# Rebuilding the last stage of a linear-attention, gated-MLP and soft-MoE kernel: turns by VectorE, experts in landing order, two output banks

## Chip, cores and metric

The kernel runs on one core of one Trainium2 chip (trn2). The metric is the device time of one execution in microseconds. The kernel before took 850.67 us, the median of three runs (848.72 to 850.92).

## What is computed

A linear attention over 8 batches of 8 heads gives x (4608 rows, 512 columns); a gated MLP with 1536 inner columns follows; and last a soft mixture of 8 experts with 4 slots each. Only the last part is touched:

```python
logits = x @ phi                              # 4608 x 32
d = softmax of logits over the 4608 rows
slot_input = d.T @ x                          # 32 x 512, 4 rows per expert
for e in range(8):
    h = np.maximum(slot_input[e] @ w1[e], 0)  # 512 -> 1024
    slot_out[e] = h @ w2[e]                   # 1024 -> 512
c = softmax of logits over the 32 slots       # the combine weights
out = c @ slot_out
```

All of it is float32. Each expert has 4 MB of weights, 33.5 MB in all, and the output is 9.4 MB.

## The kernel before, in words

The order of all instructions is written out by hand: `PROGRAM` is a list of steps such as `pair 9 2` or `piece 18`, and each mention of a step runs its generator to its next `yield`. Every engine (PE, VectorE, ScalarE, POOL, and the DMA queues of SP and POOL) works its share of this list strictly in order, so a step that waits holds back whatever stands behind it on its engine. The rows are cut into ten blocks, 0 to 7 of 512 rows and 8 and 9 of 256.

For each block, `pair(n, i)` (L591) makes one of 12 tiles of 128 inner columns of the MLP: products into g and v (L601), Silu on ScalarE (L608), product on VectorE (L610). These pairs are the bulk of PE's work. The MLP's output product is never formed: phi and w_out are folded into `wp` at the start, and `logits` (L655) takes the logits straight from the tiles hT.

`post_a` to `post_d` (L672 to L750) are the two softmaxes. `post_a` copies the logits out of PSUM, and `post_b` sums and replicates them by a product with `rep` (L690 for the last block), takes the running maximum (L697 to L701), the Exp (L705), turns the result in 32x32 blocks with VectorE into dN (L720), and turns the logits into `c_sb`, one row per token (L726). `post_d` makes the combine weights of it in place. `post_c` multiplies dN with the turned tiles hN (L763, called dh) and updates the sum U (L771).

After the last block, U is turned (`u_end`, L932), multiplied with w_out (`slot_in`, L941, tile si, 12 products of 512 columns), scaled in two halves out of one PSUM bank (L950, L952) and turned into siT (L956, L960).

The experts come next. `ex_a` (L964) multiplies siT with w1 into four column groups of one bank (L971, 256 columns), then Relu on ScalarE (L982); `ex_b` turns the result with PE (L989) and places the expert's four columns into h1T, which is zero elsewhere (L995); `ex_c` (L998) adds up y over all experts in one bank (L1007), in products of 512 columns, two column groups to a half piece. `c_stack_a` and `c_stack_b` (L781, L790) split the combine weights into a high and a low part, both twice, and turn them with PE (L798) into cT with 128 rows. `fin_a` and `fin_b` copy y, sum its four column groups by a product with `rep` (so, L1032) and split it the same way into st. `emit(k)` (L1038) then makes 512 output rows with four products of 128 rows in fp32r (L1045), copies them out alternately with ScalarE and VectorE (L1048, L1050), and writes each half, 512 KB, by SP (L1053).

The experts' weights are loaded in half pieces of 512 KB by POOL's DMA queue (`load_half`, L816; 64 in all). A piece goes where memory comes free, by the list `PLACE` (L808): `tl` is the memory of the attention stage, `hB` and `hN` are tiles of the turned blocks, `s8` are the 16 large tiles that hold the MLP's weights until the last block's pair with them is done. 44 half pieces have such a place; the other 20 are loaded into slots that an expert's product has read (`after`, L814). Before, the first pieces of this list are not the first to be loaded: the program has `piece 27` first, `piece 18` next, and pieces 0 to 4 behind that. The experts' first products run in the order 2, 4, 1, 0, 3, 7, 6, 5, their second ones in the order 0 to 7. POOL also does the last step of a weight conversion (`cv_c`, L546) and loads w_out (`wo`, L875).

Of the kernel before, what the change touches and what calls it, by code (L numbers as in the profile page):

```python
# [32 lines left out]

TS = 13

TF = 3
# [6 lines left out]
def rows(n):  # L43
# [154 lines left out]
    pd 7, pair 8 1, ua 5, qt 9 3, ub 5, pair 8 9, pair 8 1, ub 5, ub 5, x 9 1, pc 7, x 9 1, pair 8 1, uc 5, pair 8 0,  # L198
    pair 8 1, pair 8 2, pair 8 3, pair 8 4, lg 8 0, pc 7, pair 8 5, piece 27, ud 5, pair 8 9, x 9 1, x 9 1, piece 27,
    pair 8 9, x 9 1, pair 8 5, pair 8 5, pair 8 7, pair 8 5, pair 8 5, sh 8 0, pair 8 7, pair 8 7, ht 8 9, ht 8 6,  # L200
    pair 8 10, pair 8 7, wo 0, sh 8 0, lg 8 1, pair 9 2, sh 8 0, pair 8 10, pair 8 10, pair 8 11, pair 8 10, sh 8 0,
    pair 8 11, pair 8 11, pair 9 2, pair 9 2, pair 8 11, pair 9 0, pair 9 2, piece 18, piece 18, pair 8 8, pair 9 0,
    ht 8 6, piece 0, piece 4, piece 2, pair 8 8, pair 8 8, piece 25, piece 25, piece 5, pair 9 1, pair 8 8, piece 12,
    piece 3, ht 8 8, lg 8 2, piece 12, ht 8 7, piece 1, pair 9 1, pair 9 0, ht 8 7, pair 9 1, pair 9 0, ht 8 8,
    ht 8 9, pair 9 3, piece 26, pair 9 1, piece 26, ht 8 11, ht 8 10, pair 9 7, pa 8, ht 8 10, pa 8, ht 8 11,
    pair 9 7, pb 8, ht 9 0, piece 16, ht 9 2, pair 9 3, pair 9 3, pb 8, piece 16, ht 9 0, pair 9 7, pb 8, pb 8,
    pair 9 11, pair 9 7, piece 7, pair 9 3, piece 7, pb 8, pair 9 5, pb 8, pb 8, ht 9 3, lg 9 0, pd 8, pair 9 5,
    pair 9 5, pb 8, pair 9 11, pair 9 11, piece 15, pair 9 5, pd 8, piece 15, pair 9 6, pair 9 11, piece 6, pd 8,
    piece 6, pair 9 6, pair 9 6, pc 8, wo 2, pair 9 6, pair 9 4, pc 8, piece 11, piece 10, piece 9, ht 9 1, pair 9 4,
# [23 lines left out]
def kernel(  # L233
# [421 lines left out]
    def logits(n, r):  # L655
        if r == 0:
            if n < NSP:
                lg[n] = misc(name="lg0")
            else:
                lg[n] = ps.tile([128, rows(n)[1]], F32, tag="lg", bufs=1, name="lg")  # L660
        hs = h0[n, r] if n < NSP else [hT[n, 4 * r + g] for g in range(4)]
        for g in range(4):
            i = 4 * r + g
            nc.tensor.matmul(  # L664
# [333 lines left out]
    def ex_c(e):  # L998
# [3 lines left out]
        for c in range(8):  # L1002
            if c and c % 2 == 0:
                yield
# [148 lines left out]
```

## Time and profile before

| | us |
|---|---|
| median of 3 runs | 850.67 (848.72 to 850.92) |
| profiled execution, its span on the core (no other time of it is shown) | 852.4 |
| PE busy in it | 808.7 (95%) |
| VectorE, ScalarE, POOL busy | 467.6, 398.1, 257.2 |
| DMA read and written | 105.22 MB and 25.17 MB of HBM |

Times in the profile count from the first instruction of the execution. A line number is that of the kernel before. PEld is the loading of a product's stationary operand, which overlaps PE; SPq is SP's DMA queue. Where a product is in fp32, PE shows two records for it. PEclk is the granted clock of PE as a share of 2.4 GHz. Matmul ends are modelled, and busy PE is not PE at its peak.

### The profile page before, as it was taken

What the parts mean: (1) busy time and instruction counts of PE and PEld (TensorE: products, weight loads), DVE (VectorE), ACT (ScalarE), POOL (GpSimd) and SP (SyncE); (2) the same over time, 40 slices, a digit from 0 to 9 for tenths busy, and PEclk for the clock granted to TensorE, in tenths of its full rate; (3) what the DMA queues carried; (4) which work ended last, traced back from release to release, by engine and by line L of the source; (5) the groups of instructions that cost most, each with busy time, mean ns of one, the idle gap of its engine ahead of it and who ended that gap; (6) DMA issues with size and microseconds to landing.
All of it is one profiled execution on the core that took longest, in us unless ns stands there. A gap on an engine that the chain in (4) does not pass through costs nothing.

```text
span 852.4 us, 15339 instructions
## 1 busy us (share of the span) xinstructions
PE 808.7 (95%) x5823; PEld 608.2 (71%) x5823; DVE 467.6 (55%) x1024; ACT 398.1 (47%) x645; POOL 257.2 (30%) x503
## 2 busy tenths in 40 slices
PE   3799999999999999989999999999999999988983
PEld 2578778878777776767677777776786789974432
DVE  6897664366545665566468456564645372332023
ACT  5898774464524644344245225463452351432232
POOL 3333563245413323431043115101323123434200
PEclk9999999999999999999999999999999999997997
DMA  9915653352237556654465367424442346999929
GB/s 344 411 65 167 212 199 111 113 177 77 107 89 197 128 164 151 161 134 170 105 159 138 120 145 195 131 69 126 121 120 57 67 127 201 410 404 340 409 100 370
DMA packets 104073, 151.06 MB, mean 177 GB/s; under 512 B 60096, under 2 KB 73792, under 8 KB 100928
## 3 DMA queue, kind: packets, MB, share of 16 engines
q1 hardware_dynamic: 87824, 90.19, 35.1%
q0 software_dynamic: 16176, 59.90, 20.1%
q8 instruction: 46, 0.75, 0.4%
q14 instruction: 27, 0.22, 0.1%
HBM read 105.22 MB, written 25.17 MB: 153 GB/s over the span
## 4 chain that ended last, share of the span: by engine, by line
PE 88%; DMA 4%; DVE 2%; ACT 2%; SPq 2%; issue 1%; POOL 0%; DVEq 0%; ACTq 0%; POOLq 0%
PE v L601 34%; PE g L601 33%; PE dh L763 3%; PE kv L352 3%; PE lg L664 3%; PE y L1007 2%; PE px L491 2%; PE h L971 2%; PE o L1045 1%; SPq L641 1%; DMA vn<-in_vn_dram 1%; DMA kn<-in_kn_dram 1%; DMA hN<-hB 1%; DMA h0T<-hT_dr 1%; PE kmbp L337 1%
## 5 line engine op out<-in xcount | busy, mean ns | idle before, releaser
L601 PE MATMUL g<-x,W 128*128 128x512 f32 (+1 forms) x1440 | 319.2, 373 | 0.1
L601 PE MATMUL v<-x,W 128*128 128x512 f32 (+1 forms) x1440 | 318.2, 372 | 0.0
L601 PEld LDWEIGHTS g<-x,W 128*128 128x128 f32 x1440 | 249.9, 189 | 53.4 <-issue 6.9
L601 PEld LDWEIGHTS v<-x,W 128*128 128x128 f32 x1440 | 250.7, 189 | 52.1 <-issue 7.2
L610 DVE TENSOR_TENSOR hT<-hT,v 128x512 f32<-128x512 f32 (+1 forms) x120 | 75.6, 633 | 160.0 <-PE v L601 124.1
L608 ACT ACTIVATE hT<-g 128x512 f32<-128x512 f32 (+1 forms) x120 | 65.3, 555 | 164.2 <-PE g L601 126.1
L369 POOL COPY qsd<-qsd 32x16 f32<-32x16 f32 (+1 forms) x256 | 50.7, 198 | 113.1 <-DVE qsd L392 64.5
L374 POOL TENSOR_TENSOR qd<-qd,qsd 128x512 f32<-128x512 f32 (+1 forms) x64 | 59.6, 941 | 43.0 <-DVE qsd L396 10.0
L608 ACT ACT_TABLE_LOAD x52 | 66.7, 1283 | 9.4 <-PE g L601 4.3
L621 DVE STREAM_TRANSPOSE hB<-hT 128x512 f32<-128x512 f32 (+1 forms) x78 | 50.0, 671 | 9.2 <-DMA hN<-hB 8.0
L818 POOL DMA_DIRECT2D piece<-in_w_dram x55 | 29.1, 533 | 45.3 <-PE v L601 21.2
L344 ACT ACTIVATE kn<-kn 128x640 f32<-128x640 f32 x32 | 23.4, 738 | 36.1 <-DVE kn L340 33.8
L306 POOL DMA_DIRECT2D vn<-in_vn_dram x24 | 13.5, 563 | 82.7 <-PE kv L352 82.7
L501 ACT ACTIVATE x<-px 128x512 fp32r<-128x512 f32 (+1 forms) x44 | 21.1, 513 | 33.2 <-PE px L491 33.2
L312 POOL DMA_DIRECT2D qd<-in_qd_dram x24 | 13.4, 560 | 75.6 <-DVE qsT L444 71.2
L546 POOL TENSOR_TENSOR ost<-ost,f 128x1024 int32<-128x1024 int32 x9 | 21.9, 2437 | 38.4 <-DVE W L563 11.5
L340 DVE TENSOR_TENSOR kn<-kn,kmbp 128x640 f32<-128x640 f32 x32 | 25.6, 809 | 13.5 <-PE kmbp L337 13.4
L352 PEld LDWEIGHTS kv<-vn,kn 128*32 128x32 f32 x1280 | 24.6, 150 | 10.2 <-issue 7.0
L425 ACT ACTIVATE qd<-qd 128x512 f32<-128x512 f32 (+1 forms) x32 | 18.1, 577 | 26.2 <-POOL qd L374 26.0
L352 PE MATMUL kv<-vn,kn 128*32 128x65 f32 x1280 | 27.7, 240 | 1.5 <-DMA vn<-in_vn_dram 1.5
L326 DVE TENSOR_REDUCE kpart<-kn 128x128 f32<-128x640 f32 x32 | 25.8, 808 | 5.6 <-DMA kn<-in_kn_dram 3.0
L344 ACT ACT_TABLE_LOAD x16 | 20.5, 1283 | 17.0 <-DVE kn L340 16.8
(154 smaller groups left out, 892.5 us busy)
## 6 DMA issues: line engine op xcount, KB each, us to landing
piece<-in_w_dram POOLq DMA_DIRECT2D x55, 512.0 KB, 8.9
hN<-hB SPq DMA_DIRECT2D x400, 48.0 KB, 2.0
f<-in_wgv_dram SPq DMA_DIRECT2D x9, 1024.0 KB, 11.7
out_dram<-ob SPq DMA_DIRECT2D x18, 512.0 KB, 5.0
vn<-in_vn_dram POOLq DMA_DIRECT2D x24, 325.0 KB, 4.1
kn<-in_kn_dram POOLq DMA_DIRECT2D x24, 320.0 KB, 4.5
hT_dr<-hT SPq DMA_DIRECT2D x24, 256.0 KB, 2.8
ost<-in_woT_dram SPq DMA_DIRECT2D x6, 1024.0 KB, 5.2
```

Of the source, the lines that this page charges most:

```text
L326: nc.vector.tensor_reduce(out=part, in_=kn_t[b, p], axis=AX, op=ALU.max)
L340: nc.vector.tensor_tensor(out=t, in0=t, in1=mb.unsqueeze(2).to_broadcast([128, 128, ST]), op=ALU.subtract)
L344: nc.scalar.activation(out=t, in_=t, func=ACTF.Exp)
L352: nc.tensor.matmul(acc[r:r + 32, :], lhsT=ek[:, r:r + 32, i], rhs=vv[:, i, r // D, :], start=(i == 0), stop=(i == ST - 1), tile_position=( ...
L369: nc.gpsimd.tensor_copy(out=st[a:a + 32, o + 1], in_=st[b:b + 32, o])
L374: nc.gpsimd.tensor_tensor(out=a, in0=a, in1=s, op=op)
L601: nc.tensor.matmul(gv[j], lhsT=W[i][:, w, k, j, :], rhs=x[:, k, :], start=(k == 0 and w == 0 and x is xh), stop=(k == KT - 1 and w == 1),)
L608: nc.scalar.activation(out=s, in_=g, func=ACTF.Silu)
L610: nc.vector.tensor_tensor(out=s, in0=s, in1=v, op=ALU.mult)
L621: nc.vector.transpose(out=hB[n, i // w][:, :, i % w, :], in_=s.rearrange("p (b j) -> p b j", j=32))
L664: nc.tensor.matmul(lg[n][32 * g:32 * g + 32, :], lhsT=wp[:, i, :], rhs=hs[:, g] if n < NSP else hs[g], start=(r == 0), stop=(r == 2), tile ...
L818: nc.gpsimd.dma_start(out=ap, in_=(w1 if r < 4 else w2)[e, r % 4])
```

## The change

- The combine weights are no longer stacked and turned by PE (`ca`, `cb` are gone). `post_b` turns the logits so that each block of 32 columns holds every fourth row, and `post_d` turns the finished weights with VectorE in place, through an unused part of `c_sb` or `wp`. `emit` multiplies 32 rows of them with 32 rows of st in fp32, in four row groups.
- The running maximum is kept negated (`nrun`) and made in one instruction. The last block takes its Exp without an accumulator; VectorE adds the sum up afterwards. Its last tile's logits are added directly to the replicated logits (`LAST`).
- `tb`, a small Exp that loads ScalarE's table, runs behind the last Silu. `wm` gives PE four transposes of the identity at two places, without use of the result.
- si lies in two banks of 256 columns. The inner rows are turned by VectorE straight from PSUM, and Relu then writes h1T; h1T has two buffers instead of three and siT lies in `wp`.
- w2 is laid out anew on the host, so that its half pieces 0 and 1 give the left half of y and 2 and 3 the right half, each in four column groups of 256 columns. y lies in two banks, and `fin` finishes each half by itself, in fp32, without a split.
- The pieces are numbered in the order in which they are loaded: experts 0 to 7 in order, 45 half pieces with a place. Pieces 0 to 5 stand ahead of the last conversion on POOL, the experts' steps follow one another in order, and so do the output blocks. The first two blocks are written in 3 and 2 DMAs, the other seven in one of 1 MB each.

```diff
+LAST = 9
...
-    pd 7, pair 8 1, ua 5, qt 9 3, ub 5, pair 8 9, pair 8 1, ub 5, ub 5, x 9 1, pc 7, x 9 1, pair 8 1, uc 5, pair 8 0,
+    pd 7, pair 8 1, ua 5, qt 9 3, ub 5, pair 8 9, pair 8 1, ub 5, ub 5, x 9 1, piece 0, piece 1, piece 2, piece 3,
+    piece 4, piece 5, pc 7, x 9 1, pair 8 1, uc 5, pair 8 0, pair 8 1, pair 8 2, pair 8 3, pair 8 4, lg 8 0, pc 7,
...
+    pair 9 9, piece 22, piece 22, pair 9 9, tb 1, pair 9 9, pb 9, pb 9, ht 9 9, ht 9 11, wm 0, pb 9, ht 9 9, ht 9 11,
+    pb 9, pb 9, pc 9, wm 1, pb 9, pb 9, pb 9, ur, pc 9, piece 23, piece 24, piece 25, ue 0, ue 1, ue 2, ue 0, si 0,
+    ue 1, si 1, ue 2, si 2, piece 26, piece 26, piece 27, piece 27, piece 28, piece 28, pb 9, pd 9, pd 9, se, se, se,
+    se, pd 9, ea 0, ea 0, ea 0, ea 0, ea 0, ea 0, ea 0, ea 0, eb 0, eb 0, ea 1, ea 1, ea 1, ea 1, ea 1, ea 1, ea 1,
+    ea 1, eb 1, eb 1, ec 0, ec 0, ec 0, ec 0, ec 0, ec 0, ec 0, ec 0, ea 2, ea 2, ea 2, ea 2, ea 2, ea 2, ea 2, ea 2,
...
+    ec 6, ec 6, ec 7, ec 7, fin 0, ec 7, fin 0, ec 7, fin 0, fin 1, fin 1, fin 1, em 0, em 0, em 0, em 0, em 0, em 0,
...
             nc.tensor.matmul(l, lhsT=rep.bitcast(F32), rhs=lsp.pop(n), start=True, stop=False)
+            yield
+            for g in range(4):
+                nc.tensor.matmul(
+                    l[32 * g:32 * g + 32, :], lhsT=wp[:, LAST, :], rhs=hT[n, LAST],
+                    start=False, stop=True, tile_position=(0, 32 * g),
+                )
...
-            nc.vector.tensor_tensor(out=mb[:, 0:1], in0=mb[:, 0:1], in1=mrun, op=ALU.max)
-        nc.vector.tensor_scalar(out=mb[:, 2:3], in0=mb[:, 0:1], scalar1=-1.0, scalar2=None, op0=ALU.mult)
+            nc.vector.scalar_tensor_tensor(out=nm, in0=mb[:, 0:1], scalar=-1.0, in1=nrun, op0=ALU.mult, op1=ALU.min)
...
+        if n == NB - 1:
+            nc.scalar.activation(out=dT, in_=l, func=ACTF.Exp, bias=nm)
...
-            nc.vector.transpose(out=cn[r], in_=l[r].rearrange("p (t b j) -> p t b j", t=tn, b=4)[:, :, b, :])
+            nc.vector.transpose(out=cn[r], in_=l[r].rearrange("p (t j b) -> p t j b", t=tn, b=4)[:, :, :, b])
...
+        cx = c_sb[:, 32:36] if n < HB else (c_sb[:, 34:36], wp[:, 8:10])[n - HB]
         nc.vector.tensor_tensor(
-            out=cn, in0=cn, in1=cm[:, 1].unsqueeze(2).to_broadcast([128, tn, NS]), op=ALU.mult
+            out=cx, in0=cn, in1=cm[:, 1].unsqueeze(2).to_broadcast([128, tn, NS]), op=ALU.mult
         )
+        nc.vector.transpose(out=cn, in_=cx)
...
-    PLACE = ["tl"] * TL + ["hB"] + ["s8"] * TF + ["hN"] * 3 + ["s8"] * (TS - TF) + ["hN"] * 3 + ["s8"] * 3
+    PLACE = ["hA"] + ["tl"] * TL + ["s8"] * 2 + ["hB"] + ["s8"] * 7 + ["hN"] * 3 + ["s8"] * 4 + ["hN"] * 3 + ["s8"] * 3
...
+    def warm(_):
+        t = ps.tile([128, 4, 128], F32, tag="v", name="idle")
+        for j in range(4):
+            nc.tensor.transpose(t[:, j], ident, ident)
...
+            keep["si"] = [ps.tile([128, 256], F32, tag="g", name="si") for _ in range(2)]
...
     def ex_b(e):
+        t = hp.tile([128, 8, NS], F32, tag="h", name="h1_sb")
+        nc.vector.transpose(out=t, in_=h1s.pop(e).rearrange("p (c i) -> p c i", i=32))
...
+        nc.scalar.activation(out=h1T[:, :, r], in_=t[:, :, r], func=ACTF.Relu)
...
+            w = pieces[e, 4 + k]
+            for g in range(4):
+                nc.tensor.matmul(
+                    keep["y"][k // 2][32 * g:32 * g + 32, :], lhsT=keep["h1T"][:, e % 2, 4 * (k % 2) + g, :],
+                    rhs=w[:, 256 * g:256 * g + 256],
+                    start=(e == 0 and k % 2 == 0), stop=(e == NE - 1 and k % 2 == 1), tile_position=(0, 32 * g),
+                )
...
+    def fin(k):
         if k == 0:
+            keep["st"] = hp.tile([128, DM], F32, tag="h", name="st")
+        yf = hp.tile([128, DM // 2], F32, tag="h", name="yf")
+        nc.scalar.activation(out=yf, in_=keep["y"][k], func=ACTF.Copy)
+        yield
+        so = misc((128, DM // 2), "so")
+        nc.tensor.matmul(so, lhsT=rep.bitcast(F32), rhs=yf, start=True, stop=True)
+        yield
+        nc.scalar.activation(out=keep["st"][:, k * DM // 2:(k + 1) * DM // 2], in_=so, func=ACTF.Copy)
...
+        cut = ({0: 0, 1: 1, 3: 2}, {1: 0, 3: 2}, {3: 0})[min(k, 2)]
         for t in range(4):
             o = ps.tile([128, DM], F32, tag="gv"[t % 2], name="o")
-            nc.tensor.matmul(o, lhsT=ct[:, t], rhs=keep["st"], start=True, stop=True)
+            r = slice(32 * t, 32 * t + 32)
+            nc.tensor.matmul(
+                o, lhsT=c_sb[r, 4 * k:4 * k + 4, :].rearrange("s t j -> s (t j)"), rhs=keep["st"][r],
+                start=True, stop=True, tile_position=(32 * t, 0),
+            )
...
+            if t in cut:
+                r = slice(cut[t], t + 1)
+                nc.sync.dma_start(out=out[512 * k:512 * k + 512].rearrange("(p t) c -> p t c", t=4)[:, r], in_=ob[:, r])
```

## Rows read from the trace of the kernel before

**Rows 1.** The page's part 1: busy us, share of the span, instructions.
```profile
PE 808.7 (95%) x5823; PEld 608.2 (71%) x5823; DVE 467.6 (55%) x1024; ACT 398.1 (47%) x645; POOL 257.2 (30%) x503
```

**Rows 2.** Stretches: length, busy PE, PEld, DVE, ACT, POOL; PEclk; DMA share; GB/s.
```profile
700.00:720.00 20.00, 20.00 (x186) 16.99 (x186) 8.37 (x18) 5.80 (x13) 4.26 (x4) 1.00 0.54 167
780.00:800.00 20.00, 19.93 (x256) 9.74 (x248) 2.00 (x7) 6.67 (x16) 8.74 (x17) 1.00 1.01 404
```

**Rows 3.** Timeline, POOL, half pieces: start, busy, instruction, count, idle before, releaser.
```profile
720.51 2.65 POOL L818 DMA_DIRECT2D piece<-in_w_dram  x5 [11.52 <-PE v L601]
...
769.81 0.53 POOL L818 DMA_DIRECT2D hN<-in_w_dram  x1 [6.02 <-DVE c_sb L739]
...
774.71 1.05 POOL L818 DMA_DIRECT2D piece<-in_w_dram  x2 [2.83 <-PE si L941]
...
803.58 0.53 POOL L818 DMA_DIRECT2D piece<-in_w_dram  x1 [0.75 <-DMA piece<-in_w_dram]
```

**Rows 4.** As rows 2: the ends of the loads and of the outputs.
```profile
810.00:815.00 5.00, 5.00 (x36) 1.53 (x38) 0.70 (x5) 0.00 (x0) 0.00 (x0) 1.00 0.24 94
850.00:853.00 3.00, 0.00 (x0) 0.00 (x0) 0.00 (x0) 0.00 (x0) 0.00 (x0) 0.50 0.19 72
```

**Rows 5.** Timeline, 820 to 853, as rows 3: the final chain.
```profile
820.90 0.38 ACT L1027 ACTIVATE yf<-y 128x256 f32<-128x256 f32 x1 [1.31 <-PE y L1007]
821.34 1.16 PE L1032 MATMUL so<-yf,rep 128*128 128x256 f32 x4 [0.54 <-ACT yf L1027]
...
825.02 0.60 ACT L1050 ACTIVATE ob<-o 128x512 f32<-128x512 f32 x1 [1.77 <-PE o L1045]
...
826.21 20.94 SPq L1053 DMA_DIRECT2D out_dram<-ob  x18
```

**Rows 6.** Timeline, 695 to 735: the last products of the attention.
```profile
700.64 0.66 PE L491 MATMUL px<-qsT,kvs 64*64 64x256 f32 x8
```

**Rows 7.** Groups on POOL, 696 to 763.9: count, busy us, mean ns, idle before.
```profile
L818 POOL DMA_DIRECT2D piece<-in_w_dram x32 | 17.0, 534 | 29.0 <-PE v L601 21.2 <-PE lrep L694 3.3 <-PE hNp L647 3.0
L546 POOL TENSOR_TENSOR wo_st<-wo_st,f 128x1024 int32<-128x1024 int32 x1 | 2.4, 2435 | 6.0 <-ACT hT L608 6.0
...
L818 POOL DMA_DIRECT2D hN<-in_w_dram x3 | 1.6, 540 | 1.0 <-PE dh L763 1.0
```

**Rows 8.** Timeline, 735 to 783: from the last logits to the experts.
```profile
746.40 1.50 PE L763 MATMUL dh<-hN,dN 128*32 128x384 f32 x16
...
764.30 0.16 DVE L700 TENSOR_TENSOR mb<-mb,mrun 128x1 f32<-128x1 f32 x1
...
764.73 1.28 ACT L705 ACT_TABLE_LOAD   x1 [0.47 <-DVE mb L701]
...
767.75 2.79 PE L763 MATMUL dh<-hN,dN 128*32 128x384 f32 x16 [0.69 <-DVE dN L720]
...
772.45 4.65 PE L941 MATMUL si<-wo_sb,uT 128*32 128x512 f32 x24 [0.43 <-ACT uT L934]
...
779.32 3.23 PE L971 MATMUL h<-piece,h1T 128*32 128x256 f32 x56
```

**Rows 9.** Stretches of 1 us, as rows 2.
```profile
766.00:767.00 1.00, 1.00 (x4) 0.66 (x4) 0.36 (x2) 0.67 (x4) 0.00 (x0) 0.51 1.01 410
...
824.00:825.00 1.00, 0.80 (x2) 0.76 (x3) 0.06 (x1) 0.00 (x0) 0.00 (x0) 0.52 0.00 0
```

**Rows 10.** Groups by form, 779 to 824, columns as rows 7.
```profile
L1007 PE MATMUL y<-piece,h1T 128*32 128x512 f32 x96 | 18.5, 597 | 0.0
...
L1007 PE MATMUL y<-hN,h1T 128*32 128x512 f32 x32 | 6.7, 600 | 0.0
L798 PE MATMUL cTp<-ident,cs 128*128 128x128 f32 x32 | 5.0, 284 | 0.0
...
L989 PE MATMUL h1Tp<-ident,h_sb 128*128 128x128 f32 x16 | 3.3, 297 | 0.1
```

**Rows 11.** Groups by form on VectorE, whole span, columns as rows 7.
```profile
L444 DVE STREAM_TRANSPOSE qsT<-qd 128x256 f32<-128x256 f32 x8 | 3.3, 431 | 1.4 <-POOL qd L374 1.4
```

More of the change, by code (lines that the diff above doesn't have):

```diff
@@ L276 @@
     Z = per.tile([128, 1], F32, name="Z")
[L277 removed]
+    nrun = per.tile([128, 1], F32, name="nrun")
     hT_dr = tc.dram_tile([NSP, NF, 128, BLK], F32, name="hT_dr")
@@ L714, in post_b @@
             yield
-        else:
-            nc.vector.tensor_copy(out=mrun, in_=mb[:, 0:1])
-        d = sm.tile([128, tn, NS], F32, tag="dN", name="dN")
-        for b in range(4):
-            r = slice(32 * b, 32 * b + 32)
-            nc.vector.transpose(out=d[r], in_=dT[r].rearrange("p (t b j) -> p t b j", t=tn, b=4)[:, :, b, :])
-        dN[n] = d
-        yield
+        if n < NB - 1:
+            turn_d()
+            yield
+        else:
+            nc.vector.tensor_reduce(out=zb, in_=dT, axis=AX, op=ALU.add)
+            nc.vector.scalar_tensor_tensor(out=Z, in0=Z, scalar=al, in1=zb, op0=ALU.mult, op1=ALU.add)
+            yield
         cn = c_sb[:, r0 // 128:r0 // 128 + tn, :]
@@ L999, in ex_c @@
         if e == 0:
-            keep["y"] = ps.tile([128, DM], F32, tag="lg", bufs=1, name="y")
-        y = keep["y"]
-        for c in range(8):
-            if c and c % 2 == 0:
-                yield
-            w = pieces[e, 4 + c // 2].rearrange("p (c f) -> p c f", c=2)[:, c % 2]
-            g = c % 4
-            nc.tensor.matmul(
-                y[32 * g:32 * g + 32, :], lhsT=keep["h1T"][:, e % 3, c // 2, c % 2, :], rhs=w,
-                start=(e == 0 and c < 4), stop=(e == NE - 1 and c >= 4), tile_position=(0, 32 * g),
-            )
-            if c % 2:
-                ap = pieces.pop((e, 4 + c // 2))
-                j = after.get(("c", e, c // 2), 8 * NE)
-                if j < 8 * NE:
-                    yield
-                    load_half(j, ap)
@@ new lines, in ex_c @@
+        for k in range(KT):
+            if k:
+                yield
+            w = pieces[e, 4 + k]
+            for g in range(4):
+                nc.tensor.matmul(
[3 more added lines that the diff above has]
+                )
+            ap = pieces.pop((e, 4 + k))
+            j = after.get(("c", e, k), 8 * NE)
+            if j < 8 * NE:
+                yield
+                load_half(j, ap)
```

182 lines of the change are left out of this document (70 added, 112 removed).

## The prediction

> **What bounds the kernel now.** I read the page first: PE is busy 95% of the span, so the body of the kernel is PE's, and VectorE at 55% has slack there [rows 1]. The changed code is the end, so I cut that into stretches and found three limits in turn. From about 720 the weights' half pieces (512 KB each) stream at up to 404 GB/s, which makes 1.29 us for one. From 780 on PE is busy throughout while the loads run beside it [rows 2]. The last load is issued at 803.58 [rows 3], and the DMA engines go quiet at 810 + 0.24 x 5 = 811.2 [rows 4]; PE is busy with y until yf starts at 820.90 [rows 5]. That lag of 9.6 us (to 820.8, as yf waits 0.1 more) is the main thing to see: no data is missing any more, work is. After it comes a chain through yf, so, st, o and ob to the first output DMA at 826.21 [rows 5], which is 5.4 us in which nothing moves. The last stretch belongs to the DMA: 9.4 MB leave, and the data ends at 850 + 0.19 x 3 = 850.5, the span at 852.4 [rows 4]. From first issue to the end that is 26.2 us.
>
> So on this axis the end is: end of the loads + PE's lag + final chain + 26.2 us. I cost the change in these four terms. The span of the profiled execution, 852.4, is the only time shown of it; it lies 1.7 above the median of 850.67, so I carry the difference over to the median.
>
> **Term 1, the end of the loads.** Six pieces move ahead of the POOL step L546: one into the front of the h1T tile, whose memset is long over, and five into the pool that is free once the last px products are read, at 701.3 [rows 6]. POOL was idle for 6.0 us before L546, and six issues of 0.53 us [rows 7] fit in all but about 1 us of it; L546, the write of wo32 behind it on SP and the shuffles behind that move by that 1 us, and the next pieces are due at 720.51 [rows 3]. They are 7.7 us of transfer at a time when the DMA was about half used (0.54) [rows 2]. It doesn't follow that the loads end 7.7 us sooner. Before, 35 pieces were issued up to 763.8 [rows 7], and only then do slots run out: the next waits for dh of the last block, at 769.81 [rows 3]. The new list has 36 by then. With six of them gone early, the stream between 720 and 760 is limited by slots (each appears when a pair's weights are done) and idles; adding issue times and 1.29 us a piece by hand, its queue empties near 768.7, my estimate. What counts is when dh ends and how many pieces are then left: 28 instead of 29.
>
> dh of the last block moves up as follows. The Exp table load of 1.28 us leaves the chain [rows 8], since it is now issued behind the last Silu; a running maximum in one instruction instead of two saves 0.2 [rows 8]; an Exp without its accumulator saves 0.15 (two instructions of 0.2 less the sum by VectorE, which lies beside dh). The logits of the last tile go straight into the replicated sum: that takes the copy and the second product out (about 1.2) but puts two transposes and the other logits ahead of the last pair (about 0.9), both my estimates, so I count 0.3. VectorE's two hN copies now stand between maximum and transposes, 0.25 back. Sum 1.7 us. Then dh itself: 2.79 us at a granted clock that had fallen to 0.51, 1.2 GHz [rows 8, 9], against 1.50 for the same 16 records at 2.4 GHz [rows 8]. Four idle transposes are put into each of two gaps to keep the clock. I take the full clock, 1.3 to 1.4 less; so the first piece behind dh is issued at 769.8 - 3.1 = 766.7, a step that before took its rest of 29 pieces to 811.2 in 41.4 us. One piece less is 1.29, and the second gap, between the three hN pieces and the next at 774.71 [rows 3], about 1.0, goes because slot_in follows sooner: 39.1 us. **Loads end at 805.8**, 5.4 sooner.
>
> **Term 2, PE's lag.** In 779 to 824 PE gave 5.0 us to transposes of the combine weights and 3.3 to those of the inner rows [rows 10]; both go to VectorE, which had 2.0 us of work in 20 [rows 2]. y's 64 products of 512 columns took 25.2 us [rows 10] in groups of two; they become 128 of 256 columns in groups of four, the form of h: 7 groups of four in 3.23 us [rows 8], 0.46 each. All experts are then 64 x 0.46 = 29.5 us. They can begin when siT is there: before 779.32 [rows 8]; less 3.1, less 2.3 for si, 0.7 for uT and siT at full clock, 0.6 because the halves of si lie in two banks and are scaled at once: about 773 (si is 4.65 us, mostly at half clock [rows 8]). PE alone would be done at 802.5, before the loads; and since the experts are used in the order in which they land, only the last piece is left after the last landing. I give that 0.9 us, the price at half clock, because PE then waits two thirds of the time. **y ends at 806.7.** VectorE's new work here (0.43 for a turn of 128x256 [rows 11], a small memset) lies under products of the next expert; if it didn't, 0.6 us would fall on the last expert only.
>
> **Term 3, the final chain.** yf 0.38, so 0.6 to 0.9, st 0.4, about 0.4 of waits, ob 0.6 and the issue [rows 5]; VectorE's subtraction goes. The product o is new in kind: full fp32 with 32 rows, four of them in four row groups, where one fp32r product of 128 rows stood. No row shows 32x128. From below: 0.9 us for four of 512 columns, twice a group of four in h. From above: one after the other, 3.6. The nearest row is px, with 64x64 tiles in two row groups and two column groups: its eight records of 256 columns, four products, take 0.66 us [rows 6], where so needs 1.16 for two of 256 columns one after the other [rows 5]. Row groups do overlap there, and I take 0.9, doubled at half clock: PE has stood two thirds idle by then, and in the kernel before the clock fell to 0.52 in this very place [rows 9]. Chain 4.5 us instead of 5.4: **first output at 811.2.** With the full clock 3.3.
>
> The Trainium skill (TensorE: Matmul & The Clock Gate, Part 3) has four row tiles of 32 rows and 512 columns at 3.07 times one. By it the four would take 1.3 times one product, an estimate of 1.1 us instead of 0.9 at full clock, and the end would move by 0.2.
>
> **Term 4, the outputs.** 12 DMAs instead of 18, the same bytes at a rate that the DMA sets. Four products and two evacuations per engine (0.6 each by ob [rows 5], a little more on VectorE) are about 1.8 us a block at full clock, 2.4 at half, against 2.6 us that the DMA needs for it. 26.2 us stay. At half clock a bubble of 0.5 is possible behind the first block.
>
> **In the body**, each of nine blocks gets a turn of up to 128x128 on VectorE behind the combine weights (0.3 at most, the 128x256 form takes 0.43 [rows 11]) and reads its logits with a stride of four (0 to 0.3 for each of 40 turns), and loses an instruction of 0.16. VectorE's slack hides it; without cover it would be some 2 to 5 us, and nothing in the rows lets it gain.
>
> **Sum:** 5.4 + 8.7 + 0.9 = 15.0 us, span 837.4, **median 835.7**.
>
> **Rivals.**
> (a) The clock is not kept by the idle transposes: PE's clock fell at 766 [rows 9] although transposes and lrep had run just before. dh stays at 2.8, the loads end 1.4 later, the experts start at 777 and are done at 806.8, just with the loads: 837.1. For it: gaps of over 1 us remain. Against: they are shorter than the one ahead of that fall. The Trainium skill (TensorE: Matmul & The Clock Gate, Part 4) says that transposes in transpose mode don't engage the full clock as other work does; by that this rival is right, and no row parts transposes from products. Chance 0.35; it lies in my range.
> (b) The early loads bring nothing, because slots or the queue set the end: loads to 811.2 again, end 5.4 later: 841.1. For it: slots ran out before. Against: one piece less is left, and dh comes sooner. 0.12.
> (c) **The row groups of o run one behind the other.** At 0.9 us each 36 take 32.4 us; with 808.7 for the first, 0.7 for the evacuation and 5.3 for a last block of 1 MB with its end this gives a span of 847.1, median 845.4. 0.05. At half clock, 65 us: span 879, median about 878, **slower**. It decides from (852.4 - 808.7 - 6.0)/36 = 1.05 us a product. For it: no row of this form; against it px, and a PE that is always busy there would get its full clock as it has it from 780 to 800 [rows 2]. 0.04.
>
> **How the numbers follow.** The forecast has 0.44, (a) 0.35, (b) 0.12, (c) 0.09. Low end: full clock in term 3 and the loads 2 us sooner than worked out: 832. High end: it takes in (b) and a partial overlap of o: 844. Measurement can tell 0.3%, about 2.5 us. Faster 0.94, same 0.01, slower 0.05.
>
> **What would show it.** DMA share falling to nothing near 806 and first outputs within 5 us of it; PE idle with waits on pieces from about 797; the table load ahead of lrep; dh near 1.5 us; four o products within 1 to 2 us. Wrong: o's products lined up; PE busy to the end of y long after the last landing; loads still running at 811; L601's stretch longer than before.

## The result, and the profile after

The changed kernel takes 840.62 us (median of 4 runs, 838.50 to 841.73) against 850.79 (848.72 to 852.01) for the kernel before on the same chip: ratio 0.9872, 95% interval [0.9845, 0.9899]. It is faster by 10.2 us, and 15.0 had been forecast. The time lies in the forecast range (832 to 844), 4.9 us above the forecast itself.

Its profiled execution has a span of 839.7 us and took 841.44. In every profiled run of this study a time is the span plus 1.7 or 1.8. So the span of 852.4 before belongs to an execution of about 854.1, which was 3.4 us above its median, and the span after to one that was 0.8 above. Between the two profiles the gain is 12.7 us, between medians 10.2; those 2.5 us are differences between executions, and of them no profile tells more.

The stretches of the kernel after, with the columns of the stretches of before (busy time and count of PE, PEld, VectorE, ScalarE and POOL, then granted clock, DMA share, GB/s):

```profile
700.00:720.00 20.00, 19.34 (x174) 15.97 (x174) 7.92 (x18) 5.25 (x12) 6.81 (x9) 1.00 0.89 301
720.00:740.00 20.00, 20.00 (x172) 19.42 (x171) 6.17 (x21) 4.85 (x13) 6.84 (x13) 1.00 0.84 291
740.00:760.00 20.00, 20.00 (x176) 17.73 (x175) 6.49 (x22) 6.86 (x12) 7.23 (x13) 1.00 0.93 344
...
797.00:801.00 4.00, 0.61 (x12) 0.23 (x8) 0.00 (x0) 0.00 (x0) 1.59 (x3) 0.91 1.02 406
801.00:805.00 4.00, 3.50 (x32) 0.77 (x28) 0.00 (x0) 0.00 (x0) 0.00 (x0) 0.50 1.03 410
...
806.00:807.00 1.00, 1.00 (x16) 0.42 (x12) 0.06 (x2) 0.23 (x1) 0.00 (x0) 0.50 0.70 279
807.00:808.00 1.00, 1.00 (x24) 0.61 (x20) 0.00 (x0) 0.00 (x0) 0.00 (x0) 0.93 0.31 127
808.00:809.00 1.00, 1.00 (x24) 0.53 (x20) 0.00 (x0) 0.00 (x0) 0.00 (x0) 1.00 0.09 37
```

They answer to [rows 2, 4]. The early pieces fill 700 to 720 (DMA share 0.89, before 0.54), but then the DMA has holes up to 760. By its shares, put end to end, it goes quiet at 806 + 0.70 + 0.31 + 0.09 = 807.1. PE does nearly nothing from 797 to 801 and then works at half clock, 1.2 GHz, while the last pieces land.

The timeline of the kernel after (start, duration, engine, line, operation; in brackets the idle time before it and what ended it):

```profile
699.98 0.66 PE L486 MATMUL px<-qsT,kvs 64*64 64x256 f32 x8
...
702.08 2.42 PE L785 MATMUL dh<-hN,dN 128*32 128x384 f32 x25 [0.66 <-DMA hN<-hB]
...
762.68 1.28 ACT L924 ACT_TABLE_LOAD   x1
...
766.98 1.50 PE L785 MATMUL dh<-hN,dN 128*32 128x384 f32 x16 [1.40 <-DVE dN L716]
...
768.38 1.57 POOL L814 DMA_DIRECT2D hN<-in_w_dram  x3 [2.65 <-DVE rz L929]
...
770.18 2.80 PE L947 MATMUL si<-wo_sb,uT 128*32 128x256 f32 x48 [0.37 <-ACT uT L938]
...
774.62 0.64 PE L976 MATMUL h<-h1T,wp 128*32 128x256 f32 x8 [0.39 <-DVE wp L965]
...
800.66 2.26 PE L976 MATMUL h<-piece,wp 128*32 128x256 f32 x16 [3.39 <-DMA piece<-in_w_dram]
...
805.26 4.13 PE L1006 MATMUL y<-piece,h1T 128*32 128x256 f32 x56
809.53 0.70 PE L1024 MATMUL so<-yf,rep 128*128 128x256 f32 x2
810.16 0.64 PE L1006 MATMUL y<-piece,h1T 128*32 128x256 f32 x8
811.36 0.70 PE L1024 MATMUL so<-yf,rep 128*128 128x256 f32 x2 [0.56 <-ACT yf L1021]
812.54 1.14 PE L1035 MATMUL o<-st,c_sb 32*128 32x512 f32 x8 [0.47 <-ACT st L1026]
...
814.32 16.40 SPq L1047 DMA_DIRECT2D out_dram<-ob  x12
```

Against [rows 5, 6, 8]: dh takes 1.50 us instead of 2.79 and si 2.80 instead of 4.65, both at full clock. PE waits 3.39 us ahead of expert 7. Four products of o take 1.14 us. One group of y stands behind the first half of so. A new wait is at 702.08: dh of block 7 waits for hN. The first pieces behind dh of the last block are issued at 768.38.

Executions differ by 3 to 4 us in the body of the kernel ahead of all this, so times of different profiles are compared from the start of px, the last products of the attention (700.64 before, 699.98 after), as "px + ...". The loads' end is the point where the DMA's shares, put end to end, run out, as above; a single piece can land later than that, as e11 shows below. Each ratio is to the kernel before, run beside it on the same chip.

| kernel | loads' end | first output issue | end of span | median, us | ratio to before |
|---|---|---|---|---|---|
| before | px + 110.6 | px + 125.6 | px + 151.8 | | |
| after | 107.1 | 114.3 | 139.7 | 840.62 | 0.9872 [0.9845, 0.9899] |
| e1_c6_first | 107.7 | 116.5 | 145.3 | 839.90 | 0.9867 [0.9841, 0.9893] |
| e2_piece0_behind | 106.1 | 114.4 | 139.8 | 839.38 | 0.9859 [0.9830, 0.9888] |
| e3_no_warm | 107.3 | 115.4 | 140.7 | 840.28, one run | |
| e4_ballast | 107.5 | 116.3 | 141.6 | 841.04 | 0.9886 [0.9861, 0.9910] |
| e6_early_undone | 107.5 | 114.4 | 139.7 | 838.77 | 0.9862 [0.9844, 0.9881] |
| e7_no_table | 107.9 | 114.3 | 139.7 | 838.94, one run | |
| e8_tail_bare | 105.8 | 113.5 | 141.2 | 841.94 | 0.9886 [0.9857, 0.9915] |
| e8_tail_filled | 106.2 | 113.9 | 139.3 | 838.66 | 0.9854 [0.9836, 0.9872] |
| e9_o_serial | | 113.9 | 178.6 | 880.55, one run | |
| e10_dh_late | 111.4 | 117.3 | 142.6 | 842.41 | 0.9901 [0.9882, 0.9921] |
| e11_tail_kept | 105.8 | 112.7 | 138.1 | 837.08 | 0.9840 [0.9824, 0.9856] |
| e12_both | 110.6 | 121.1 | 147.9 | 847.99 | 0.9974 [0.9956, 0.9991] |

The medians of one kernel's runs spread over 3 us or more, so among the kernels near 840 the distances from px carry the argument, and the ratios say whether the whole bears them out.

### The profile page after: what moved, and what is told of

Read it like the earlier page. It is cut to its first block, busy times and chain, and to the rows that moved or that the text cites. A ratio compares the mean times of both kernels' runs of the same rounds, so it can differ in the third digit from the quotient of the medians.

```text
span 839.7 us, 15603 instructions
## 1 busy us (share of the span) xinstructions
PE 798.2 (95%) x5973; PEld 605.6 (72%) x5973; DVE 466.6 (56%) x1013; ACT 389.2 (46%) x626; POOL 256.5 (31%) x503
## 4 chain that ended last, share of the span: by engine, by line
PE 81%; DMA 9%; SPq 4%; DVE 2%; ACT 1%; issue 1%; POOL 1%; DVEq 0%; ACTq 0%; POOLq 0%
PE v L596 33%; PE g L596 32%; DMA piece<-in_w_dram 4%; SPq L636 3%; PE kv L347 3%; PE dh L785 3%; PE lg L662 3%; PE o L1035 2%; PE px L486 2%; DMA vn<-in_vn_dram 1%; DMA hN<-hB 1%; DMA h0T<-hT_dr 1%; DMA kn<-in_kn_dram 1%; DMA wo<-wo_st 1%; PE kmbp L332 1%
## 5 line engine op out<-in xcount | busy, mean ns | idle before, releaser
L347 PEld LDWEIGHTS kv<-vn,kn 128*32 128x32 f32 x1280 | 24.6, 149 | 10.2 <-issue 7.0
L498 DVE TENSOR_TENSOR x<-px,x 128x512 fp32r<-128x512 f32 (+1 forms) x44 | 24.5, 583 | 7.3 <-ACT x L496 7.1
```

Of the source, the lines that this page charges most:

```text
L347: nc.tensor.matmul(acc[r:r + 32, :], lhsT=ek[:, r:r + 32, i], rhs=vv[:, i, r // D, :], start=(i == 0), stop=(i == ST - 1), tile_position=( ...
```

## The experiments

**Where the loads' gain comes from.** The DMA in the 15 us around dh and si, first of the kernel before, then of the kernel after (stretches, columns as above):

```profile
766.00:781.00 15.00, 12.61 (x91) 5.31 (x95) 5.51 (x23) 2.32 (x10) 5.26 (x10) 0.66 0.88 312
```

```profile
766.00:781.00 15.00, 13.09 (x199) 7.68 (x203) 6.78 (x28) 2.00 (x8) 6.81 (x13) 1.00 1.01 405
```

Before, (405 - 312) x 15 us = 1.4 MB were not moved there, 3.4 us of transfer: the queue ran dry. After, there is no hole, and that is the 3.5 us by which the loads end sooner. The change offers two causes: six pieces loaded early, and a shorter chain through dh and si. Four runs part them. (A third, one more place for a piece, stays in all runs and so is not tested.) The first puts the six pieces back.

```diff
-    x 9 1, piece 0, piece 1, piece 2, piece 3, piece 4, piece 5, pc 7,
+    x 9 1, pc 7,
...
-    pair 9 2, piece 7, piece 7, pair 8 8,
+    pair 9 2, piece 7, piece 7, piece 0, piece 1, piece 2, piece 3, piece 4, piece 5, pair 8 8,
```

> The six early pieces (0 to 5) are issued behind piece 7 again, at about px + 22 us instead of around px; nothing else moves. Theory: the early issue is worth next to nothing. In the changed kernel the DMA had some 8 us of idle time between px + 20 and px + 50 and was full from px + 52 to the end of the loads, so 7.7 us of transfers that come 25 us later find room in it; the loads end within 1 us of px + 107 as before, block 7's dh runs without its 0.7 us wait, and the time is that of the changed kernel within 0.2%, 839.5 to 842. Prediction's step: the early issue sets one piece and the queue ahead of dh, so the loads end about 1.3 later: 842. Rival: all six pieces count, the DMA was short by 7.7 us: loads end at px + 114, time 846 to 848.

Timeline of this kernel (36 pieces are issued ahead of dh here too, the last four at 759.21):

```profile
696.80 0.66 PE L485 MATMUL px<-qsT,kvs 64*64 64x256 f32 x8
...
759.21 2.09 POOL L813 DMA_DIRECT2D piece<-in_w_dram  x4 [4.52 <-PE v L595]
...
762.55 1.50 PE L784 MATMUL dh<-hN,dN 128*32 128x384 f32 x16 [1.39 <-DVE dN L715]
```

Loads' end, first output and end stand nearly where they stood (px + 107.5, 114.4, 139.7), and the median is no worse. In the changed kernel, then, the early issue brings next to nothing: much of what it moves at px + 0 to 20 is missing as holes at px + 20 to 60, since the free slots are the limit there (POOL's issues of pieces wait for the products v that read the memory). But dh of the last block comes at px + 65.8 here and at 67.0 in the changed kernel, so the early issue also has a price, which the next run shows: piece 0 alone goes behind the five others.

```diff
-    x 9 1, piece 0, piece 1, piece 2, piece 3, piece 4, piece 5, pc 7,
+    x 9 1, piece 1, piece 2, piece 3, piece 4, piece 5, piece 0, pc 7,
```

> The changed kernel with piece 0, the one in the front of the h1T tile, issued behind pieces 1 to 5 instead of ahead of them. Theory: piece 0 at 696.4 runs beside the last shuffles of block 7 and holds up the rows that dh of that block needs; PE stood idle near 701 for about 1.4 us. Expected: no wait of dh on the shuffle, every slot from 720 on comes 1.4 us sooner, and so do the end of the loads and the end: 1 to 1.5 us less. Rival: that wait is there anyway (another transfer, or the five pieces at 701), and the trace still shows PE idle near 701; no change of the end.

Timeline of this kernel, dh of block 7 and dh of the last block:

```profile
698.33 0.66 PE L486 MATMUL px<-qsT,kvs 64*64 64x256 f32 x8
698.92 2.79 PE L785 MATMUL dh<-hN,dN 128*32 128x384 f32 x32
...
763.87 1.50 PE L785 MATMUL dh<-hN,dN 128*32 128x384 f32 x16 [1.40 <-DVE dN L716]
```

The first runs in one go, where in the kernel after it waited for `hN<-hB`: piece 0, issued at 696.37 there, had run beside the small shuffles that dh needs. (Of the eight kernels with piece 0 in front seven have this wait, 0.46 to 0.79 us; e12 hasn't. None of the four with it behind has.) The next slots come at px + 19.9 instead of px + 21.3, dh of the last block at px + 65.5 instead of 67.0, and the loads end 1.0 sooner.

So the early pieces aren't worthless. Against e6, whose dh comes nearly as early, the loads end 1.4 sooner here, and the three kernels below that also have piece 0 behind agree (px + 105.8 to 106.2). The early issue is worth about 1.4 us of the loads' end, and the wait on piece 0 takes about 1.0 of it away. The end of the kernel follows neither (139.7 and 139.8): PE is the later of the two in the tail.

The other cause was tried from two sides: 1.28 us put back ahead of dh, and 8 us put in behind it.

```diff
-    pair 9 9, tb 1, pair 9 9,
+    pair 9 9, pair 9 9,
```

> The early load of the Exp table is taken out, so ScalarE loads it between the last logits and Exp again, 1.28 us. Prediction's step: dh comes 1.3 later, so the first piece behind it, the end of the loads and the end: 842 instead of 840.6. Theory: dh starts at px + 68.3 instead of px + 67.0, but the DMA's queue holds some 4 us of transfers when dh ends, so the DMA share stays at 1 and the loads end at the same distance from px (within 0.5); PE's wait ahead of expert 7 takes the 1.3 us up; the end stays at px + 139.7 within 0.7.

dh came 1.3 later (px + 68.3), the loads ended 0.8 later and the end was exactly where it was, px + 139.7. So the early table load is worth nothing by itself in this kernel.

```diff
-    pb 9, pb 9, pb 9, ur, pc 9,
+    pb 9, pb 9, pb 9, ur, wm 2, wm 3, wm 4, wm 5, wm 6, wm 7, wm 8, wm 9, wm 10,
+    wm 11, wm 12, wm 13, wm 14, wm 15, pc 9,
```

> Fourteen times four idle transposes (0.57 us for four, 8.0 in all, 6.5 of it beyond what PE waits anyway) stand ahead of dh of the last block, so dh starts near px + 73.5 instead of px + 67.0, and all behind it. Prediction's step (dh's time decides the end of the loads): loads and end 6.5 later, 847. Theory: the queue holds about 4 us when dh ends, so the DMA has a hole of 2 to 3 us after px + 72, the loads end 2 to 3 us later, and PE, with 28 us of experts' work from px + 81, ends y near px + 111 to 113: end px + 140.5 to 142.5, time 841.5 to 843.5.

The idle steps fell behind dh, not ahead of it as the expectation has it (dh is part of the step before): dh stays at px + 66.8, uTp comes 5.8 later, and si and the experts 5.5. Timeline and stretches of this kernel:

```profile
766.11 6.77 PE L919 MATMUL idle<-ident 128*128 128x128 f32 x60
772.72 0.49 PE L936 MATMUL uTp<-ident,U 128*128 128x128 f32 x3
```

```profile
768.00:772.00 4.00, 4.00 (x39) 4.00 (x38) 0.51 (x3) 0.00 (x0) 0.00 (x0) 1.00 1.00 373
772.00:776.00 4.00, 3.63 (x60) 2.43 (x57) 0.00 (x0) 0.76 (x4) 1.03 (x2) 1.00 0.26 101
776.00:780.00 4.00, 3.44 (x56) 2.21 (x52) 1.71 (x7) 0.47 (x1) 3.14 (x7) 1.00 0.88 305
```

The hole is back: (405 - 101) x 4 + (405 - 305) x 4 = 1.6 MB, 4.0 us, and the loads end 4.3 later. A delay of 1.3 ahead of dh gave 0.8, one of 5.5 to 5.8 behind it 4.3, so the queue covers some 0.5 to 1.5 us of it and not the 4 that I had expected. The chain through dh and si does decide the end of the loads, as the prediction said. The end of the kernel moved by 2.9 only, because PE waits less ahead of expert 7 (1.55 us instead of 3.39).

**Does less work on PE pay?** 13 idle steps, 52 transposes with 8.5 us of busy PE in this trace, are put among experts 0 to 4; the change had removed 48 transposes with 8.3 us [rows 10].

```diff
-    ec 0, ec 0, ea 2,
+    ec 0, ec 0, wm 2, wm 3, wm 4, ea 2,
...
-    ec 4, ea 6,
+    ec 4, wm 13, wm 14, ea 6,
```

> The changed kernel with 13 more idle steps on PE (52 transposes of the identity, as many as the change took away in turns of combine weights and inner rows), spread behind the second products of experts 0 to 4. At about 0.6 us a step they are 7 to 8 us of PE work. Theory: with the experts in order of landing PE has slack and the loads set the end, so the removal of PE's transposes as such is worth nothing now: the end within 1 us of 839.7, perhaps sooner because PE does not idle. Rival: the removed PE work made the gain; the end comes 6 to 8 us later.

The end moves by 1.9 us (px + 141.6), the median by 0.4. PE's wait ahead of expert 7, which is gone here, took most of it up, and PE then ran at a clock of 1.00 to the end of y. So neither the expectation (within 1 us) nor its rival (6 to 8) was met. That isn't the whole truth either, as the last run shows, which has both this ballast and the late chain (the diff shows the first steps of each):

```diff
-    pb 9, pb 9, pb 9, ur, pc 9,
+    pb 9, pb 9, pb 9, ur, wm 15, wm 16,
...
-    ec 0, ec 0, ea 2,
+    ec 0, ec 0, wm 2, wm 3, wm 4, ea 2,
```

> Two earlier edits together: the 13 idle steps of four transposes among experts 0 to 4 (7.4 us of PE work, about what the transposes took that the change removed) and the 14 idle steps in the chain behind dh of the last block, which put the start of the experts off by 5.8 us. Alone they moved the end by some 2 and 3 us against px. Theory: each was covered by PE's slack ahead of the last pieces, and that cover is there only once. PE starts the experts at px + 80.5 and has 28 + 7.4 us of work, so y ends at px + 116 to 117.5, the first output comes at px + 119.7 to 121, the end is at px + 145 to 147: time 846 to 848.5, most of the way back to the kernel before. Rival (the end is the loads' end, moved by the hole in the DMA alone): as with the late chain alone, end px + 142.6, time 842 to 843.

```profile
810.37 3.21 PE L1006 MATMUL y<-piece,h1T 128*32 128x256 f32 x56
...
818.49 16.39 SPq L1047 DMA_DIRECT2D out_dram<-ob  x12
```

In the timeline of this kernel, whose px starts at 697.43, y ends near 815.0, which is px + 117.5, though the loads end at px + 110.6: a lag of PE of 7 us is back. End px + 147.9, 847.99 us, as worked out. Alone the two edits cost 1.9 and 2.9, together 8.2: each hid in the same wait of PE ahead of expert 7, which is there only once and is gone in this run. Less PE work and an early start of the experts were both needed, and neither shows its worth alone.

**The clock around dh.** The two idle steps that were to keep it are taken out (one execution).

```diff
-    ht 9 11, wm 0, pb 9, ht 9 9, ht 9 11, pb 9, pb 9, pc 9, wm 1, pb 9,
+    ht 9 11, pb 9, ht 9 9, ht 9 11, pb 9, pb 9, pc 9, pb 9,
```

> The changed kernel without the two idle steps around dh of the last block. Theory: they keep the clock; without them it falls near 766 as before, dh takes 2.8 us instead of 1.5 and si 4.6 instead of 2.8, the experts start 4 us later, and the end moves by 0 to 1.5 us since the DMA queue is full meanwhile. Rival (the page's rule that such transposes do not engage the clock): the steps do nothing, the clock stays at full without them as well because the gaps are shorter than before, dh 1.5 and si 2.8 us as they are.

```profile
764.00:768.00 4.00, 2.35 (x20) 0.92 (x20) 3.38 (x16) 0.54 (x4) 1.57 (x3) 1.00 1.00 401
...
764.80 1.50 PE L785 MATMUL dh<-hN,dN 128*32 128x384 f32 x16 [1.83 <-DVE dN L716]
```

Timeline of the kernel before:

```profile
765.96 1.10 PE L798 MATMUL cTp<-ident,cs 128*128 128x128 f32 x4 [1.94 <-DVE cs L788]
```

In the stretch of e3, which holds dh, the clock is 1.00 without them too, dh takes 1.50 us and si 2.80. The kernel before stood at 0.51 in the same place [rows 9]. PE was idle there for 1.94 us (ahead of a turn of the combine weights) and 0.69 us (ahead of dh), here for 1.83, and in e7_no_table, which kept 1.00 as well, for 2.67 at a stretch. What let the clock fall before and not here stays open. In this one execution it wasn't the idle steps that kept it; whether others would lose it without them was not tested.

**The tail.** PE waits ahead of expert 7 while expert 6's last products, whose pieces are there, stand behind. So they go ahead.

```diff
-    ea 7, ea 7, ea 7, ea 7, eb 7, eb 7, ec 6, ec 6, ec 6, ec 6, ec 7,
+    ec 6, ec 6, ec 6, ec 6, ea 7, ea 7, ea 7, ea 7, eb 7, eb 7, ec 7,
```

> The changed kernel with the second product of expert 6 put ahead of the first product of expert 7 on PE; nothing else moves. Theory: the lag of 3.8 us between the last landing (807.0) and the end of y (810.8) is PE work in the wrong place: expert 6's four groups, whose weights landed before 800, stand behind expert 7's first product, which waits for landings until 804.4, and so for the left half of y stands ahead of the last group. Expected: PE's idle stretch of 3.4 us before 800.6 is filled with these groups, y ends about 1 us after the last landing instead of 3.8, the end comes 2 to 3 us sooner, near 837. Rival: the last pieces' landing sets the end and the order is free; then y still ends more than 3 us after the last landing and the end stays within 0.5 us of 839.7 on the trace.

Timeline:

```profile
806.76 1.22 PE L1024 MATMUL so<-yf,rep 128*128 128x256 f32 x2
...
811.25 2.09 PE L1035 MATMUL o<-st,c_sb 32*128 32x512 f32 x8 [0.47 <-ACT st L1026]
```

The wait is filled, but PE then waits piece by piece at a clock of 0.50, which doesn't come back: so takes 1.22 us a half, four products of o 2.1, and the outputs go at PE's pace to px + 145.3. Neither the theory nor the rival had the clock. This execution took 844.44, at a mean granted clock of 0.972 over its span; the other five took 839.2 to 842.4 at 0.979 to 0.989, so it doesn't always go that far. The same order, with piece 0 behind, and with the first half of so behind the last group of y (against the changed kernel):

```diff
-    piece 0, piece 1, piece 2, piece 3, piece 4, piece 5, pc 7,
+    piece 1, piece 2, piece 3, piece 4, piece 5, piece 0, pc 7,
...
-    ea 7, ea 7, ea 7, ea 7, eb 7, eb 7, ec 6, ec 6, ec 6, ec 6,
-    ec 7, ec 7, fin 0, ec 7, fin 0, ec 7, fin 0, fin 1, fin 1, fin 1,
+    ec 6, ec 6, ec 6, ec 6, ea 7, ea 7, ea 7, ea 7, eb 7, eb 7,
+    ec 7, ec 7, fin 0, ec 7, ec 7, fin 0, fin 1, fin 0, fin 1, fin 1,
```

> Piece 0 behind pieces 1 to 5, expert 6's inner product ahead of expert 7's first, and so of the first half behind expert 7's last group. Theory: PE waits piece by piece for the last eight pieces, so its granted clock stands at about 0.5 from there; y ends about 2 us behind the last landing, so takes 1.2 us, four products of o over 2 us, and the outputs go at PE's speed: end near px + 140 to 144, time 839 to 843, no better than the changed kernel. Rival: order is all that counts, the clock is back in time: y ends within 1 us of the last landing (px + 107), first output at px + 111, end near px + 136.5, time 837.

Its stretches:

```profile
800.00:802.00 2.00, 1.14 (x16) 0.17 (x11) 0.00 (x0) 0.00 (x0) 0.00 (x0) 1.00 1.03 410
802.00:804.00 2.00, 0.97 (x8) 0.16 (x8) 0.50 (x2) 0.09 (x1) 0.00 (x0) 0.65 1.03 410
804.00:806.00 2.00, 1.81 (x16) 0.47 (x16) 0.00 (x0) 0.14 (x1) 0.00 (x0) 0.50 0.85 340
...
828.00:832.00 4.00, 4.00 (x14) 2.26 (x12) 1.64 (x3) 2.04 (x4) 0.00 (x0) 0.50 0.84 346
```

PE was about half busy up to 804 and the clock went to 0.50. It came back for a moment and fell again; at 828 PE is busy throughout and still at 0.50. The first output is 0.8 us sooner than after, and the outputs lose more than that. Not in every execution, though: three took 841.8 to 843.2 us at a mean granted clock of 0.973 to 0.978, and one took 837.12 at 0.993, the time that the rival gives the better order. That points to the clock as what the order alone lacks. Now four idle transposes behind each of seven groups of expert 7 (against the kernel just shown):

```diff
-    ea 7, ea 7, ea 7, ea 7, eb 7, eb 7, ec 7, ec 7, fin 0, ec 7, ec 7,
+    ea 7, wm 2, ea 7, wm 3, ea 7, wm 4, ea 7, wm 5, eb 7, eb 7,
+    ec 7, wm 6, ec 7, wm 7, fin 0, ec 7, wm 8, ec 7,
```

> The kernel with the same three moves, and seven times four idle transposes put on PE between the groups of expert 7, which wait for their pieces. Theory: what keeps PE busy keeps its clock, transposes too; the granted clock stays at 1.00 through y, so 0.7 us, four products of o 1.14 us, y ends within 1 us of the last landing, first output near px + 111, end near px + 136.5: 837, some 3 to 4 us under the changed kernel. Rival (transposes don't hold the clock): it stands at about 0.5 as without them, each four take 1.2 us and stand in y's way: y ends 2 to 4 us behind the last landing and the time is 841 to 845, above the kernel without the idle steps.

The clock had fallen already when they began (0.58 at 800 to 802, after two waits of 0.6 among expert 6's groups), was 1.00 from 804 to the last product, and y ended at px + 110.3, 3 us later than forecast, since PE had fallen behind and the idle steps stood in its way. Neither theory had that, and 838.66 us is above the 837 of the first. So they start earlier and stop earlier (against the kernel just shown):

```diff
-    ec 6, ec 6, ec 6, ec 6, ea 7, wm 2, ea 7, wm 3, ea 7, wm 4, ea 7, wm 5, eb 7, eb 7,
-    ec 7, wm 6, ec 7, wm 7, fin 0, ec 7, wm 8, ec 7,
+    ec 6, ec 6, wm 2, ec 6, wm 3, ec 6, wm 4, ea 7, wm 5, ea 7, wm 6, ea 7, wm 7, ea 7, wm 8, eb 7, eb 7,
+    ec 7, wm 9, ec 7, fin 0, wm 10, ec 7, ec 7,
```

> Piece 0 behind pieces 1 to 5, expert 6's inner product ahead of expert 7's first, so behind the last group, and nine times four idle transposes from the second group of expert 6 on, one behind each group that is followed by a wait, none ahead of the last. Theory: the clock stays at 1.00 from px + 96 on (in the kernel filled only from expert 7 on it had fallen to 0.58 before the first of them, and PE ran behind by 3 us); y ends within 1.2 us of the last landing, first output near px + 112.5, end near px + 138, time 838 to 839.3, the fastest so far by a little. Rival (the fillers cost PE more than the clock gives): y ends 2 us or more behind the last landing as it did there, end px + 139.3 or later, time as of the kernel filled late, 838.7, or above.

Stretches and timeline:

```profile
796.00:804.00 8.00, 7.57 (x80) 3.47 (x72) 0.50 (x2) 0.23 (x1) 0.53 (x1) 1.00 0.90 358
804.00:806.00 2.00, 1.41 (x20) 0.67 (x20) 0.00 (x0) 0.38 (x1) 0.00 (x0) 1.00 0.07 27
...
816.00:820.00 4.00, 4.00 (x20) 2.01 (x20) 2.77 (x5) 2.25 (x4) 0.00 (x0) 1.00 1.04 430
```

```profile
805.90 0.64 PE L1006 MATMUL y<-piece,h1T 128*32 128x256 f32 x8 [0.59 <-DMA piece<-in_w_dram]
806.47 1.33 PE L1024 MATMUL so<-yf,rep 128*128 128x256 f32 x4
808.28 1.14 PE L1035 MATMUL o<-st,c_sb 32*128 32x512 f32 x8 [0.47 <-ACT st L1026]
```

The clock is 1.00 from 796 until the outputs, the last group of y starts when its piece lands, and the end is at px + 138.1. All four executions stood at a mean granted clock of 0.991 to 0.994, where of the same order without idle steps one in four did. At 837.08 us this is the fastest kernel of the study, 0.9840 [0.9824, 0.9856]; the intervals of this ratio and of the changed kernel's overlap by a little.

**Do the row groups of o overlap?** All four products of a block take rows 0 to 31 (three quarters of the output rows are then computed from the wrong rows).

```diff
-    o, lhsT=c_sb[r, 4 * k:4 * k + 4, :]..., rhs=keep["st"][r],
-    start=True, stop=True, tile_position=(32 * t, 0),
+    o, lhsT=c_sb[0:32, 4 * k:4 * k + 4, :]..., rhs=keep["st"][0:32],
+    start=True, stop=True, tile_position=(0, 0),
```

> All four products of o of a block read rows 0 to 31 and use the first row group, so that they can't overlap (three quarters of the output's rows are then computed from the wrong rows). Theory: the four overlapped before (1.14 us); one behind the other they take 3.4 to 3.8 us at the full clock, 36 of them 31 to 34 us, more than the 23 us that the DMA needs: the outputs become PE's, last product near px + 144 to 147, time 848 to 852, as the prediction's third rival had it. Rival: the products ran one behind the other already, each in 0.3 us, and nothing changes: 1.1 to 1.2 us for four, time 840.

```profile
840.00:860.00 20.00, 20.00 (x25) 7.70 (x24) 4.14 (x6) 3.58 (x6) 0.00 (x0) 0.50 0.38 157
```

This stretch has 25 records in 20 us, two to a product: 1.6 us for one, at half clock though PE is busy throughout. At full clock that makes an estimate of 3.2 us for four, against the 1.14 of the changed kernel: there the four do overlap. The expectation had the full clock and so missed the time (848 to 852). The span of 878.8 is the one that the prediction's rival had for half clock (879), but partly by luck: the products started at 812.3 instead of 808.7, and took 60.6 us instead of 65. The rival's price was about right; in the changed kernel it just wasn't paid.

## Why the prediction was right, and where it was off

Forecast, from the same px: end at 837.4 - 700.6 = px + 136.8. Measured: px + 139.7.

- **Term 1, the loads** (5.4 sooner forecast, 3.5 measured). That the chain through dh and si sets their end was right: e10 puts the hole and 4.3 us back. From the first piece behind dh to the loads' end the forecast had 39.1 us, and 38.7 were measured (39.2 in e2, 40.3 in e6 without the early pieces). The step that failed is the one before: that piece was to be issued 3.1 sooner than before and was issued 0.8 sooner (px + 68.4 against 69.2). dh became 1.3 shorter as forecast, but it starts at px + 67.0 against 67.1 before, and not 1.7 sooner. The chain itself was nearly right in size: dh starts at px + 65.5 in e2 and 65.8 in e6. It was lost again because piece 0 makes dh of block 7 wait, for which the prediction has no term. I had looked for that collision on POOL's and SP's queues, and it was among the transfers. Whether one piece less is worth 1.29 wasn't tested by itself, as e6 also has 36 pieces issued ahead of dh. Rival (b), that the early loads bring nothing, comes out in the changed kernel (0.4 against e6), but its sum was wrong, as the loads ended 3.1 sooner without them, and so was its reason, as e2 against e6 shows.
- **Term 2, PE's lag** (0.9 forecast, 3.7 measured, 9.6 before). This is the step that is off most, by 2.8 us. "The experts are used in the order in which they land, only the last piece is left" is not what the list says: four groups of expert 6 stand behind expert 7's first half, they run at half clock, and the first so stands ahead of the last group. And the last landing is later than the point where the DMA goes quiet: in e11 PE waits for the last piece until 805.90, while the point worked out from the shares is 803.1; from 804 to 806 the mean share is 0.07, about one of 16 engines. I took the one for the other. Before, PE's lag hid it. Of the 9.6, e12 brings back 7 with PE work and a late start alone (end 8.2 later, against 1.9 for the ballast by itself); how the experts' order and the new form of y share in the rest no run tells.
- **Term 3, the chain** (4.5 forecast, 3.5 measured). From 810.8 to 814.32, at full clock, for which the prediction had 3.3. The choice of half clock was wrong here and right in e1 and e8_tail_bare. Four products of o take 1.14 us: the 0.9 was too low. The Trainium skill (TensorE: Matmul & The Clock Gate, Part 3) has 3.07 times for four row tiles; with 0.9 for one product that is an estimate of 1.17, which the prediction gave as 1.1. The measurement agrees to within a tenth: by e9's 1.6 us at half clock one product is an estimate of 0.8 at full clock, so the four gain 2.8 times.
- **Term 4, the outputs** (26.2 forecast, 25.4 measured): PE's work is hidden behind the DMA as said, as long as the clock is full. In e1, at 0.50, PE takes them over. What 12 DMAs instead of 18 have to do with the 0.8 wasn't tested.
- **The body** paid nothing beyond the 1.4 us of the collision: PE is still busy 20.00 of 20 us from 720 to 760.
- **The sum**: 1.9 + 2.8 - 1.0 - 0.8 is the 2.9 us between px + 136.8 and 139.7. The other 2 us of the miss in the median lie between executions. To call the span "1.7 above the median" was a mistake of meaning: a span was set against times. As times, the execution profiled before was 3.4 above its median and the one after 0.8, so the difference that was carried over did not stay the same.

Rival (a) held that transposes don't keep the clock. The clock stayed, but e3 shows that it stays without them, so its outcome was wrong and its reason wasn't tested at that place. It was tested elsewhere: in e10 PE ran nothing but transposes from 766.1 to 772.7 at 1.00, and e11 keeps with them a clock that e8_tail_bare loses. The Trainium skill (TensorE: Matmul & The Clock Gate, Part 4) has it that transpose mode doesn't engage the full clock; for these fp32 transposes of the identity, if they run in that mode (the profile writes them as MATMUL), the measurement decides against it as far as keeping the clock goes. No run here shows transposes alone raising it.

## What to carry to other kernels

Two ends that lie close together, here the last landing and PE's last product, hide each other's gains: try edits in pairs before calling one worthless. When PE has to wait piece by piece at the end, look at the granted clock behind the wait, not only at the wait; a few idle transposes in the gaps, begun before the clock falls and none ahead of the last group, were worth more than the better order alone (ratio 0.9840 [0.9824, 0.9856] against 0.9886 [0.9857, 0.9915]). And an early prefetch has to be checked for what its transfers run beside: here it was worth 1.4 us of the loads' end, and its first piece cost 1.0 of them by a wait in the very chain that the change made shorter.

## Not expected of the hardware

- The same products of o, with PE busy 4.00 of 4 us, ran at a granted clock of 1.00 in e11 (816 to 820) and at 0.50 in e8_tail_bare (828 to 832). A full queue of work didn't bring the clock back there, nor in e9 (20 us of such a stretch are shown).
- Nothing but transposes kept PE at 1.00 for 6.6 us (e10).
- The last of a stream of 512 KB loads landed 2.8 us after the end that the mean DMA shares give (e11), with about one of the 16 engines still at work.
- A 512 KB load issued beside the small `hN<-hB` shuffles delayed a product that needs them by 0.7 us in one wait, and the slots and dh of the last block behind it by 1.4 (after against e2).
